# Spreading late weight loads, deeper output and row buffers, two PSUM bank moves and a split last copy in an attention-plus-experts kernel

## The chip, the cores and the metric

One Trainium2 chip, one core. The metric is the device time of one execution in microseconds (us), lower is better. Times come from repeated executions; a profile is one execution with the hardware profiler on, and its span (first to last instruction) is about 1.8 us shorter than the time of the same execution. Most executions of one kernel lie close together.

## The reference, cut to what matters

```python
# attention: batch 4, 8 heads, 768 positions, head_dim 64; each query sees 8 global keys and 96 local ones,
# with a distance bias per head; softmax; then the heads are laid side by side: x is [3072 tokens, 512]
def _moe_ref(x, w_gate, w1, w2):          # 8 experts, w1 [8,512,1024], w2 [8,1024,512]
    cap = N // E                          # 384 tokens for each expert, exactly
    logits = x @ w_gate
    order = np.argsort(-logits.flatten()) # best (token, expert) pair first
    ...                                   # greedy: a pair is taken if the token is free and the expert has room
    for e in range(E):
        h = np.maximum(x[mask_e] @ w1[e], 0.0)
        out[mask_e] = h @ w2[e]
```

## The kernel before

Three memories matter: HBM (the chip's large memory), SBUF (the core's working memory) and PSUM (where TensorE's products land, in banks). The kernel runs in three stages: attention (to about 142 us), routing (the selection of 384 tokens for each expert by rounds, to about 175 us; TensorE does early expert work in its gaps), and the expert stage. In the expert stage the rows of an expert are gathered from HBM by index in slabs of 128 (`xe`), transposed on TensorE (`pxe`), copied to SBUF by VectorE (`xT`), multiplied by w1 (`ph`, ReLU on ScalarE into `hT`) and by w2 (`po`), copied to an output buffer by VectorE (`ot`) and scattered to the output rows. Gathers, scatters and the 1 MB weight loads are all issued by GpSimd and share one DMA queue. Experts 0 to 3 have one slab done early and 2 slabs left; experts 4 to 7 have 3 slabs.

```python
    gp = ...tile_pool(name="gp", bufs=9)     # gathered rows xe
    op = ...tile_pool(name="op", bufs=4)     # output buffers ot
    def late_weights(pin=True):              # next pending 1 MB load: w1_5, w2_5, w1_6, w2_6, w1_7, w2_7
        if lates:
            dst, s_ = lates.pop(0)
            ins = nc.gpsimd.dma_start(dst, s_)
            if pin: tc.keep_in_program_order(ins)
    # ... cut ...
    # end of routing: gathers of experts 0 to 3, then two loads
            for e in range(EX):
                gather(e, range(1, TSLAB), False)
            for _ in range(2):
                late_weights(False)
    # ... cut: expert stage, first=True ...
            load_x(0)                        # transposes and row copies of expert 0
            for e in range(N_EXP):
                ahead = 3
                if e + ahead < N_EXP and not (first and e + ahead < EX):
                    gather(e + ahead, slabs(e + ahead))
                if first and e in (2, 3):
                    late_weights()
                    late_weights()
                # up: ph (3 banks), ReLU to hT
                if e + 1 < N_EXP:
                    load_x(e + 1)
                for j, t in enumerate(slabs(e)):
                    po = ps_o.tile([128, DM], FP32, tag="po")         # 3 banks
                    for fc in range(NFC):
                        nc.tensor.matmul(po, lhsT=hT[...], rhs=w2_of(e)[:, fc, :], ...)
                    ot = op.tile([128, DM], FP32, tag="ot")
                    nc.vector.tensor_copy(out=ot, in_=po)
                    scatter(ot, idi[:, ...])
```

One round of the selection, the part that the change touches. `pk` and the counts `pn` lie in one tile, so in one PSUM bank:

```python
            pkn = ps_d.tile([128, 512], FP32, tag="pk")
            pk = pkn[:, 0:256]...
            # TensorE writes pk, then
            pn = pkn[:, 256:257]
            for hf in range(2):
                nc.tensor.matmul(pn, lhsT=nb[...], rhs=ones_bf[:, 0:1], ...)
            nc.scalar.activation(Xe[:, nk : nk + 1], pn, AF.Identity, scale=-1.0, bias=bias232)
            work(0.85)                                   # TensorE's filler: early expert work
            nc.vector.max(out=mx8, in_=pkn[:, 0:256])    # MAX8
            # Xe from mx8 ... then pr on TensorE from Xe
```

The early output of experts 0 to 3 (`down_one`) accumulates in `pos[e] = ps_f.tile(..., tag="po")`, one bank for all four.

The softmax here doesn't subtract the row's maximum and nothing guards it: scores larger than these inputs give would overflow.

Of the kernel before, what the change touches and what calls it, by code (L numbers as in the profile page):

```python
# [9 lines left out]
FP32 = mybir.dt.float32  # L10
# [10 lines left out]
DM = H_ * D_  # L21
N_EXP = 8
# [6 lines left out]
TSLAB = CAP // 128  # L29
# [16 lines left out]
def kernel(  # L46
# [12 lines left out]
    nc = tc.nc  # L59
# [214 lines left out]
    with ExitStack() as actx:  # L274
# [143 lines left out]
        po = {}  # L418
# [462 lines left out]
    xctx = ExitStack()  # L881
# [7 lines left out]
    w2pool = ctx.enter_context(tc.tile_pool(name="w2pool", bufs=1, reuse_waits="tile"))  # L889
    w_late[2] = w_2  # L890
    late_tiles(w2pool, range(3, N_EXP - 2))
    gp = xctx.enter_context(tc.tile_pool(name="gp", bufs=9, reuse_waits="tile"))
    fp = xctx.enter_context(tc.tile_pool(name="fp", bufs=2, reuse_waits="tile"))
    hp = xctx.enter_context(tc.tile_pool(name="hp", bufs=2, reuse_waits="tile"))
    op = xctx.enter_context(tc.tile_pool(name="op", bufs=4, reuse_waits="tile"))

    def late_weights(pin=True):
        if lates:
            dst, s_ = lates.pop(0)
            ins = nc.gpsimd.dma_start(dst, s_)  # L900
            if pin:
                tc.keep_in_program_order(ins)
# [34 lines left out]
    def early_work(ps_f):  # L937
        hTs, phs, pos = {}, {}, {}
        items = []

        def rows(e):
            def go():
                px = ps_f.tile([128, NKC, 128], BF16, tag="ph", bufs=2, name=f"px{e}")
                for kc in range(NKC):
                    nc.tensor.transpose(px[:, kc, :], xe_early[e][:, 128 * kc : 128 * kc + 128], ident_bf)
                nc.scalar.copy(out=xT_early[e], in_=px)
            items.append((0.25, go))

        def up_one(e, f4, i):
            def go():  # L950
                if f4 == 0 and i == 0:
                    if e % 3 == 0:
                        hTs[e // 3] = hp.tile([128, NFC, CAP], BF16, tag="hT", name=f"hTE{e}")
                if i == 0:
                    phs[e, f4] = ps_f.tile([128, 4, 128], FP32, tag="ph", bufs=2, name=f"phE{e}_{f4}")
                sub, kc = divmod(i, NKC)
                fc = 4 * f4 + sub
                nc.tensor.matmul(phs[e, f4][:, sub, :], lhsT=w1_of(e)[:, kc, 128 * fc : 128 * fc + 128],
                                 rhs=xT_early[e][:, kc, :], start=(kc == 0), stop=(kc == NKC - 1), skip_group_check=True)
                if i == 4 * NKC - 1:  # L960
                    nc.scalar.activation(hTs[e // 3][:, 4 * f4 : 4 * f4 + 4, 128 * (e % 3) : 128 * (e % 3) + 128],
                                         phs[e, f4], AF.Relu)
            items.append((0.078, go))

        def up(e):
            for f4 in range(NFC // 4):
                for i in range(4 * NKC):
                    up_one(e, f4, i)

        def down_one(e, fc):  # L970
            def go():
                if fc == 0:
                    pos[e] = ps_f.tile([128, DM], FP32, tag="po", name=f"poE{e}")
                nc.tensor.matmul(pos[e], lhsT=hTs[e // 3][:, fc, 128 * (e % 3) : 128 * (e % 3) + 128], rhs=w2_of(e)[:, fc, :],
                                 start=(fc == 0), stop=(fc == NFC - 1))
                if fc == NFC - 1:
                    ot = op.tile([128, DM], FP32, tag="ot", name=f"otE{e}")
                    nc.scalar.copy(out=ot, in_=pos[e])
                    nc.gpsimd.memset(nop, 0.0)
                    scatter(ot, idiE[:, e : e + 1])  # L980
            items.append((0.22, go))

        def down(e):
            for fc in range(NFC):
                down_one(e, fc)

        for e in range(EX):
            rows(e)
        for f, e in ((up, 0), (up, 1), (down, 0), (up, 2), (down, 1), (up, 3), (down, 2), (down, 3)):
            f(e)  # L990
        return items

    def routing(general):
      with ExitStack() as dctx:
        dap = dctx.enter_context(tc.tile_pool(name="dap", bufs=1))
        ditp = rpool
        ps_d = dctx.enter_context(tc.tile_pool(name="ps_d", bufs=1, space=bass.MemoryType.PSUM, reuse_waits="tile"))
# [56 lines left out]
        def fast_round(k, X, Dg):  # L1054
            nk = 16 * k
            UB = best(X, Dg)
            pkn = ps_d.tile([128, 512], FP32, tag="pk", name="pkn")
# [8 lines left out]
            for hf in range(2):  # L1066
                nc.tensor.matmul(pk[:, hf, :], lhsT=nb[:, 128 * hf : 128 * hf + 128], rhs=neg_bf,
                                 start=False, stop=True, skip_group_check=True)
            pn = pkn[:, 256:257]
            for hf in range(2):  # L1070
                nc.tensor.matmul(pn, lhsT=nb[:, 128 * hf : 128 * hf + 128], rhs=ones_bf[:, 0:1],
                                 start=(hf == 0), stop=(hf == 1), skip_group_check=True)
            if X is None:
# [7 lines left out]
                out=Xe[:, 0:nk].rearrange("p (c k) -> p c k", k=k),  # L1081
                in0=XM.rearrange("p (c o) -> p c o", o=1).to_broadcast([128, 16, k]),
                in1=mx8[:, 0:k].rearrange("p (o k) -> p o k", o=1).to_broadcast([128, 16, k]),
                op=ALU.mult)
            tok_end()
            pr = ps_d.tile([128, 129], FP32, tag="pr", name="pr")
            nc.tensor.matmul(pr[:, 0 : nk + 1], lhsT=Gm, rhs=Xe[:, 0 : nk + 1], start=True, stop=True)
            prk = ps_d.tile([128, 512], FP32, tag="pr2", name="prk")
            pr2, rk = prk[:, 0:128], prk[:, 128:256]
            nc.tensor.matmul(pr2[:, 0:nk], lhsT=Gm, rhs=Xe[:, 0:nk], start=True, stop=True,  # L1090
                             skip_group_check=True)
            X = begin_X()
# [3 lines left out]
            for k0 in range(0, k, 4):  # L1096
                nc.vector.tensor_tensor(
                    out=tg[:, k0 : k0 + 4, 0:nk],
# [184 lines left out]
        if True:  # L1283
            work(0.7)
            X, Dg = None, None
            for kk in ROUND_KS:
                X, Dg = fast_round(kk, X, Dg)
            best(X, Dg)
            work(1.1)
            mnf = rpool.tile([128, NCHUNK], FP32, tag="mnf", name="mnf")  # L1290
            nc.vector.tensor_tensor(out=mnf, in0=mn, in1=cflag, op=ALU.subtract)
            nc.vector.tensor_tensor(out=M, in0=Ub[:, 8:32, :], in1=bc_e(mnf), op=ALU.is_le)
            dispatch()
            for e in range(EX):
                gather(e, range(1, TSLAB), False)
            for _ in range(2):
                late_weights(False)
            vt = rpool.tile([128, EC, EX], BF16, tag="vt", name="vt")
            for lo_, hi_, at in ((16, 32, 0), (8, 10, 16)):
                n_ = hi_ - lo_  # L1300
                nc.vector.tensor_tensor(
                    out=vt[:, at : at + n_, :], in0=Ub[:, lo_:hi_, 0:EX], op=ALU.is_gt,
                    in1=mn[:, lo_ - 8 : hi_ - 8].rearrange("p (c o) -> p c o", o=1).to_broadcast([128, n_, EX]))
            nc.vector.tensor_tensor(out=vt, in0=vt, in1=Ck, op=ALU.mult)
            work(1.0)
            pf = ps_d.tile([128, 512], FP32, tag="pk", name="pf")
            nc.tensor.matmul(pf[0:1, 0:CE], lhsT=ones_bf[:, 0:1], rhs=Mf, start=True, stop=True, skip_group_check=True)
            nc.tensor.matmul(pf[0:1, CE : CE + EX * EC], lhsT=ones_bf[:, 0:1], rhs=vt.rearrange("p c e -> p (c e)"),
                             start=True, stop=True, skip_group_check=True)
            fc8 = dap.tile([1, N_EXP + 1], FP32)  # L1310
            nc.vector.tensor_reduce(out=fc8[:, 0:N_EXP], in_=pf[0:1, 0:CE].rearrange("p (c e) -> p e c", e=N_EXP),
                                    axis=AX.X, op=ALU.add)
            nc.vector.tensor_tensor(out=fc8[:, 0:N_EXP], in0=fc8[:, 0:N_EXP], in1=capv, op=ALU.subtract)
            nc.vector.tensor_tensor(out=fc8[:, 0:N_EXP], in0=fc8[:, 0:N_EXP], in1=fc8[:, 0:N_EXP], op=ALU.mult)
            nc.vector.tensor_reduce(out=fc8[:, N_EXP : N_EXP + 1], in_=pf[0:1, CE : CE + EX * EC], axis=AX.X, op=ALU.add)
            fm = dap.tile([1, 1], FP32)
            nc.vector.tensor_reduce(out=fm, in_=fc8, axis=AX.X, op=ALU.max)
            nc.vector.tensor_single_scalar(out=fi, in_=fm, scalar=0.0, op=ALU.is_gt)
            while items:
                work(0.1)  # L1320
            while deferred:
                tok_begin()
                tok_end()

    def experts(first):
        with ExitStack() as fctx:
# [23 lines left out]
            for e in range(N_EXP):  # L1350
# [2 lines left out]
                ahead = 3 if first else 2  # L1353
                if e + ahead < N_EXP and not (first and e + ahead < EX):
                    gather(e + ahead, slabs(e + ahead))
                if first and e in (2, 3):
                    late_weights()
                    late_weights()
                hT = hp.tile([128, NFC, CAP], BF16, tag="hT")
                for fc in range(NFC):  # L1360
# [8 lines left out]
                for j, t in enumerate(slabs(e)):  # L1369
                    po = ps_o.tile([128, DM], FP32, tag="po")  # L1370
                    for fc in range(NFC):
                        nc.tensor.matmul(po, lhsT=hT[:, fc, 128 * j : 128 * j + 128],  # L1372
                                         rhs=w2_of(e)[:, fc, :], start=(fc == 0), stop=(fc == NFC - 1))
                    ot = op.tile([128, DM], FP32, tag="ot")
                    nc.vector.tensor_copy(out=ot, in_=po)  # L1375
                    scatter(ot, idi[:, TSLAB * e + t : TSLAB * e + t + 1])

    routing(False)
# [51 lines left out]
```

## Time and profile before

| | before |
|---|---|
| time, median of 4 runs (range) | 277.33 us (276.89 to 279.37) |
| span of the profiled execution (its time) | 274.4 us (276.2) |
| TensorE busy | 245.6 us, 90% |
| expert 5 to expert 6, start to start | 20.76 us |
| expert 6 to expert 7 | 11.07 us |

In the page, the busy row has 40 equal slices of the span with the busy share in tenths; PEclk is the granted clock of TensorE in tenths. From the page of the kernel before:

```profile
span 274.4 us, 7770 instructions
...
PE 245.6 (90%) x3299; PEld 179.0 (65%) x3299; DVE 163.4 (60%) x346; ACT 142.1 (52%) x240; POOL 87.6 (32%) x145
...
PE   8699899999999999999988889979999994499970
...
PEclk9999999999999999999999999999999999599995
```

TensorE is full but for a hole in slices 34 and 35 (226 to 240 us), with a slower clock just behind it. Its timeline there (columns: start us, duration us, engine, line, operation, output<-inputs, shape, count, and in brackets the idle time before it and what ended it):

```profile
223.25 5.36 PE L1363 MATMUL ph<-xT,w 128*128 128x384 bf16 x32
...
237.23 0.59 PE L1341 MATMUL pxe<-ident_bf,xe 128*128 128x128 bf16 x4 [7.73 <-DMA out_dram<-ot,idi]
237.61 6.57 PE L1372 MATMUL po<-w,hT 128*128 128x512 bf16 x22
244.01 5.36 PE L1363 MATMUL ph<-xT,w 128*128 128x384 bf16 x32
...
255.08 5.37 PE L1363 MATMUL ph<-xT,w 128*128 128x384 bf16 x32
```

L1363 with 32 matmuls is one expert's first product: the starts give the step of an expert. The transposes of expert 6 (L1341) wait 7.73 us. The wait is inherited from VectorE, whose timeline says why:

```profile
223.77 1.34 DVE L1375 COPY ot<-po 128x512 f32<-128x512 f32 x2 [4.64 <-DMA out_dram<-ot,idi]
236.15 0.69 DVE L1375 COPY ot<-po 128x512 f32<-128x512 f32 x1 [11.04 <-DMA out_dram<-ot,idi]
236.76 0.74 DVE L1342 COPY xT<-pxe 128x512 bf16<-128x512 bf16 x2
```

An output copy waits 11.04 us for a buffer that an earlier scatter still reads; the row copies (L1342) behind it in VectorE's order wait along, and TensorE waits for them. GpSimd's timeline shows where that scatter stood:

```profile
216.37 0.85 POOL L900 DMA_DIRECT2D w<-in_moe_w_dram  x1
218.69 0.93 POOL L900 DMA_DIRECT2D w<-in_moe_w_dram  x1 [1.46 <-issue]
223.82 1.04 POOL L931 DMA_INDIRECT out_dram<-ot,idi  x1 [4.21 <-DMA out_dram<-ot,idi]
```

The scatter was issued at 223.82 behind two loads; its completion is in the trace at 236.03, 12.2 us later, where scatters in an empty queue need 2.7 us. It had also been issued late: its rows were in the buffer at 211.34 (expert 3's first output copy), but GpSimd, which works in program order, first issued another scatter, three gathers and the two loads and then waited 4.21 us for an earlier scatter, which was itself 13.5 us in the queue (210.19 to 223.65) behind the pair of loads issued at 208.08 and 208.90.

One round of the selection, from the timelines of ScalarE and VectorE: MAX8 waits for ScalarE's read of the counts, though it uses nothing of it.

```profile
152.06 0.26 ACT L1076 ACTIVATE Xe<-pkn,bias 128x1 f32<-128x1 f32 x1
```

```profile
152.35 0.43 DVE L1079 MAX8 mx<-pkn 128x8 f32<-128x256 f32 x1 [0.92 <-ACT Xe L1076]
```

And the end of the kernel:

```profile
260.28 5.34 PE L1372 MATMUL po<-w,hT 128*128 128x512 bf16 x24
...
265.66 0.69 DVE L1375 COPY ot<-po 128x512 f32<-128x512 f32 x1 [1.03 <-PE po L1372]
266.63 0.97 POOL L931 DMA_INDIRECT out_dram<-ot,idi  x1 [0.76 <-DVEq L1387]
```

### The profile page before, as it was taken

How to read it: one execution, taken by the hardware profiler on the slowest of the kernel's cores; microseconds unless marked ns; L12 is line 12 of the kernel's file. 1: busy time of each engine (PE TensorE's matmuls, PEld its weight loads, DVE VectorE, ACT ScalarE, POOL GpSimd, SP SyncE). 2: the span in 40 equal slices, each digit the busy share in tenths (PEclk: the TensorE clock that was granted, in tenths of full speed). 3: DMA queues.
4: the chain of work that ended last, by engine and by line, in shares of the span. 5: the costliest groups of instructions: out<-in, count | busy, mean ns of one | idle time of the engine just before them, and what ended most of it. 6: DMA issues, size and time to landing. Idle time of an engine off the chain costs nothing. (4 is left out here: it accounts for less than half of the span.)

```text
span 274.4 us, 7770 instructions
## 1 busy us (share of the span) xinstructions
PE 245.6 (90%) x3299; PEld 179.0 (65%) x3299; DVE 163.4 (60%) x346; ACT 142.1 (52%) x240; POOL 87.6 (32%) x145
## 2 busy tenths in 40 slices
PE   8699899999999999999988889979999994499970
PEld 2567688888898888878876756656666652145520
DVE  3978998888969887798647677612143210233130
ACT  5998969596895959734332222234333523023500
POOL 5050000020713940050081001478448637141240
PEclk9999999999999999999999999999999999599995
DMA  7993889499597999589969998148976999820321
GB/s 268 327 270 77 205 211 273 85 222 261 124 281 146 237 217 200 127 128 211 209 136 179 208 214 167 60 112 148 191 279 116 186 267 208 279 91 24 117 80 44
DMA packets 52569, 49.29 MB, mean 180 GB/s; under 512 B 29744, under 2 KB 44080, under 8 KB 52528
## 3 DMA queue, kind: packets, MB, share of 16 engines
q0 software_dynamic: 15680, 26.22, 46.4%
q1 hardware_dynamic: 36848, 22.50, 32.5%
q8 instruction: 28, 0.46, 0.8%
q14 instruction: 13, 0.11, 0.1%
HBM read 56.05 MB, written 9.44 MB: 239 GB/s over the span
## 5 line engine op out<-in xcount | busy, mean ns | idle before, releaser
L1366 ACT ACTIVATE hT<-ph 128x256 bf16<-128x256 f32 (+1 forms) x64 | 27.9, 437 | 51.8 <-PE ph L1363 50.1
L400 ACT ACTIVATE P<-ps 128x860 f32<-128x860 f32 (+1 forms) x46 | 39.3, 895 | 23.2 <-PE ps L382 22.5
L382 PE MATMUL ps<-qT,kA 32*128 32x215 f32 (+2 forms) x864 | 43.6, 333 | 2.1 <-ACT qT L347 2.1
L435 PE MATMUL po<-P,v 128*64 128x215 f32 (+6 forms) x576 | 41.5, 293 | 0.3 <-DVE P L415 0.3
L382 PEld LDWEIGHTS ps<-qT,kA 32*128 32x128 f32 x864 | 37.2, 185 | 6.8 <-issue 2.8
L435 PEld LDWEIGHTS po<-P,v 128*64 128x64 f32 x576 | 33.9, 136 | 8.7 <-issue 3.2
L1375 DVE COPY ot<-po 128x512 f32<-128x512 f32 x20 | 13.7, 692 | 43.4 <-PE po L1372 21.1
L415 DVE TENSOR_TENSOR P<-P,Wm 128x860 f32<-128x860 f32 (+1 forms) x32 | 32.9, 1043 | 6.6 <-ACT P L400 3.9
L931 POOL DMA_INDIRECT out_dram<-ot,idi x20 | 19.7, 984 | 37.8 <-DVE ot L1375 31.0
L322 DVE STREAM_TRANSPOSE RT<-RT 128x768 f32<-128x768 f32 x28 | 26.2, 958 | 3.3 <-DMA RT<-in_k_dram 3.3
L466 PE MATMUL pr<-P,onesx 128*32 128x192 f32 (+11 forms) x768 | 27.6, 259 | 0.0
L1372 PE MATMUL po<-w,hT 128*128 128x512 bf16 x112 | 27.3, 397 | 0.0
L1372 PEld LDWEIGHTS <-hT 128*128 128x128 bf16 x160 | 15.6, 100 | 17.5 <-issue 2.2
L466 PEld LDWEIGHTS pr<-P,onesx 128*32 128x32 f32 x768 | 24.7, 109 | 2.3 <-issue 0.3
L1363 PE MATMUL ph<-xT,w 128*128 128x384 bf16 (+1 forms) x160 | 25.1, 316 | 0.0
L332 ACT COPY kA<-RT 128x720 f32<-128x720 f32 (+2 forms) x18 | 24.4, 1354 | 0.1
L1342 DVE COPY xT<-pxe 128x512 bf16<-128x512 bf16 x20 | 7.8, 420 | 24.8 <-PE pxe L1341 24.3
L1363 PEld LDWEIGHTS <-w 128*128 128x128 bf16 x160 | 15.6, 98 | 9.3
L923 POOL DMA_INDIRECT xe<-x_tok,idi x20 | 19.2, 961 | 7.1 <-issue 4.6
L408 DVE TENSOR_TENSOR P<-P,Wm 128x860 f32<-128x860 f32 x16 | 16.4, 1058 | 7.1 <-ACT P L400 7.1
L440 ACT COPY oT<-po 128x384 f32<-128x384 f32 x32 | 14.8, 490 | 11.1 <-PE po L435 11.1
L511 PE MATMUL pk<-ident,oT 128*128 128x128 f32 x96 | 16.5, 288 | 2.1 <-DVE LT L482 2.0
(230 smaller groups left out, 316.4 us busy)
## 6 DMA issues: line engine op xcount, KB each, us to landing
w<-in_moe_w_dram POOLq DMA_DIRECT2D x10, 1024.0 KB, 14.0
v<-in_v_dram SPq DMA_DIRECT2D x32, 180.0 KB, 3.8
RT<-in_k_dram SPq DMA_DIRECT2D x7, 768.0 KB, 4.4
RT<-in_q_dram SPq DMA_DIRECT2D x7, 768.0 KB, 7.3
w_early<-in_moe_w_dram POOLq DMA_DIRECT2D x8, 512.0 KB, 7.9
x_tok<-x SPq DMA_DIRECT2D x32, 96.0 KB, 3.3
RT<-in_moe_w_dram POOLq DMA_DIRECT2D x2, 1024.0 KB, 16.9
w_early<-in_k_dram SPq DMA_DIRECT2D x1, 768.0 KB
```

The lines of the kernel that those rows point to most:

```text
L322: nc.vector.transpose(out=t, in_=src[:, :, 32 * g : 32 * g + 32])
L332: nc.scalar.copy(out=kA[:, i0:i1, 8:128].rearrange("p i (c j) -> p i c j", j=NJ), in_=t[:, i0 * NC5 : i1 * NC5, :].rearrange("p (i c) j -> ...
L382: nc.tensor.matmul(heads[a][:, o : o + w], lhsT=kA[r, gd, i, :], rhs=qTt[r, gd, KT * i : KT * i + w], start=(gd == 0), stop=(gd == 1), ski ...
L400: nc.scalar.activation(P[:, :, 0 : GW[g]], ps[w_][:, :, 0 : GW[g]], AF.Exp, scale=0.125)
L415: tt(out=P[:, :, 0 : GW[g]], in0=P[:, :, 0 : GW[g]], in1=Wm[:, h0 : h0 + 2, lo : lo + GW[g]], op=ALU.mult)
L435: nc.tensor.matmul(po[n][bk][64 * t : 64 * t + 64, a - QB * bk : z - QB * bk], lhsT=v7[:, t, i, :], rhs=P[:, t, o + a - q0 : o + z - q0], ...
L466: nc.tensor.matmul(o_, lhsT=l_, rhs=r_, start=first[gq], stop=True, skip_group_check=True)
L923: ins = nc.gpsimd.indirect_dma_start(out=xe, out_offset=None, in_=x_tok[:, :], in_offset=bass.IndirectOffsetOnAxis(ap=idi[:, s : s + 1], a ...
L931: s = nc.gpsimd.indirect_dma_start(out=out[:, :], out_offset=bass.IndirectOffsetOnAxis(ap=ids, axis=0), in_=ot, in_offset=None)
L1363: nc.tensor.matmul(ph[:, 0 : 128 * ns], lhsT=w1_of(e)[:, kc, 128 * fc : 128 * fc + 128], rhs=xT_e[:, kc, 0:ns, :].rearrange("p t n -> p (t ...
L1366: nc.scalar.activation(hT[:, fc, 0 : 128 * ns], ph[:, 0 : 128 * ns], AF.Relu)
L1372: nc.tensor.matmul(po, lhsT=hT[:, fc, 128 * j : 128 * j + 128], rhs=w2_of(e)[:, fc, :], start=(fc == 0), stop=(fc == NFC - 1))
```

## The change

The intent: no burst of loads in the queue in front of scatters; more buffers, so that a late scatter holds up nobody; MAX8 free of ScalarE; no wait of expert 3's early accumulator for expert 2's copy; the last copy shared by two engines.

```diff
-    gp = xctx.enter_context(tc.tile_pool(name="gp", bufs=9, reuse_waits="tile"))
+    gp = xctx.enter_context(tc.tile_pool(name="gp", bufs=11, reuse_waits="tile"))
-    op = xctx.enter_context(tc.tile_pool(name="op", bufs=4, reuse_waits="tile"))
+    op = xctx.enter_context(tc.tile_pool(name="op", bufs=6, reuse_waits="tile"))
@@ early output of experts 0 to 3
-                    pos[e] = ps_f.tile([128, DM], FP32, tag="po", name=f"poE{e}")
+                    pos[e] = ps_f.tile([128, DM], FP32, tag="pt" if e == 2 else "po", name=f"poE{e}")
@@ one round of the selection
-            pn = pkn[:, 256:257]
+            prk = ps_d.tile([128, 512], FP32, tag="pr2", name="prk")
+            pr2, rk, pn = prk[:, 0:128], prk[:, 128:256], prk[:, 256:257]
@@ (the allocation of prk further down goes)
@@ end of routing
-            for _ in range(2):
-                late_weights(False)
+            late_weights(False)
@@ expert stage
-                if first and e in (2, 3):
-                    late_weights()
+                if first:
                     late_weights()
@@
-                    nc.vector.tensor_copy(out=ot, in_=po)
+                    if e == N_EXP - 1 and t == TSLAB - 1:
+                        nc.vector.tensor_copy(out=ot[:, 0 : DM // 2], in_=po[:, 0 : DM // 2])
+                        nc.scalar.copy(out=ot[:, DM // 2 : DM], in_=po[:, DM // 2 : DM])
+                    else:
+                        nc.vector.tensor_copy(out=ot, in_=po)
```

More of the change, by code (lines that the diff above doesn't have):

```diff
@@ L1087, in fast_round @@
             nc.tensor.matmul(pr[:, 0 : nk + 1], lhsT=Gm, rhs=Xe[:, 0 : nk + 1], start=True, stop=True)
-            prk = ps_d.tile([128, 512], FP32, tag="pr2", name="prk")
-            pr2, rk = prk[:, 0:128], prk[:, 128:256]
             nc.tensor.matmul(pr2[:, 0:nk], lhsT=Gm, rhs=Xe[:, 0:nk], start=True, stop=True,
```

## The prediction

> **What bounds the kernel now.** Time 277.3 us, profiled span 274.4. The engine table has TensorE busy 245.6 us (90%); the 40 slices show it near full except at 230-237 us and in the last slices. The chain of waits is useless here (two pieces, 0.5%), so I read the timeline of TensorE. From 182 us on it runs expert after expert without a gap, except one idle stretch of 7.73 us before 237.23 (released, says the trace, by an output scatter). One expert of 3 slabs takes 11.07 us (starts at 212.18, 223.25; 244.01, 255.08), but from 223.25 to 244.01 it takes 20.76: 9.7 us lost, of which about 1.7 is half clock after the pause (clock records: 0.5 from 234.1 to 241.0; 22 matmuls took 6.57 us instead of 4.91).
>
> Why: VectorE's timeline has an output copy that waits 11.04 us for the scatter that last used its buffer (4 buffers, next to a 4.64 us wait just before); the row-transposing copies for the next expert stand behind it in order, and TensorE behind those. That scatter was issued at 223.82 and landed at 236.03, against 2.7 us in an empty queue, because two weight loads (1 MB each, about 6 us of queue time each, issued 216.4 and 218.7) were ahead of it in the one GpSimd queue. The Trainium skill (DMA: Bandwidth & Descriptors, "Two DMAs through the same engine are not ordered") says descriptors of a queue start in order; the landings here agree.
>
> **The change.**
> 1. Late loads one by one, behind each expert's gathers, and 6 output buffers. I replayed the queue by hand (estimate: weights 6 us, scatter 0.65, gather 0.33, and the eight-deep reuse of completion semaphores): weights of experts 6 and 7 land near 210, 218, 226 and 235, and are wanted from about 232, 237, 243 and 248; no output copy waits for a scatter. Gain 9.7 us, all on TensorE's path.
> 2. Row counts in another bank. MAX8 in each of 4 selection rounds now waits for the ScalarE read of the same bank (0.76 to 0.95 us idle, released by ScalarE); the built program makes it wait for TensorE instead. It saves one handover and a 0.26 us activation: about 0.35-0.4 us a round, 1.4 us in all. TensorE idles 0.35-0.71 us for this chain in each round, so it counts.
> 3. Expert 2's early accumulator in another bank: TensorE's 0.67 us wait at 178.7 goes.
> 4. Last copy in halves. Both halves read one bank. The Trainium skill (PSUM — Partial Sum Buffer, "PSUM bank collisions raise a hardware error") says two engines must not read one bank at once; the built program agrees: the ScalarE half waits for VectorE. They run in series: estimate 0.43 + 0.38 + handover 0.1 against 0.69, so 0.2 us lost.
> 5. Two more row buffers: gathers of expert 4 no longer wait for TensorE; nothing on the path.
>
> Sum: 9.7 + 1.4 + 0.7 - 0.2 = 11.6 us.
>
> **Predicted: 265.7 us, range 263.5 to 268.5.** Faster by over 2% 0.95, within 2% 0.04, slower 0.01.
>
> **What the profile would show.** Span near 262.8. Every 3-slab expert 11.1 us apart, no TensorE wait above 1 us after 182; no half clock before the end. VectorE's wait for scatters gone from the list of waits (15.7 us now). MAX8 released by TensorE, gathers starting near 174.1 instead of 175.6. The last copies one after the other, TensorE's end to last scatter about 0.2 longer. Busy times of engines nearly unchanged.
>
> **What would make it wrong.** A late weight arriving late (the last one has about 13 us of slack by the replay); a new stall of GpSimd on a completion semaphore held by a weight load, which delays scatters or gathers; selection gains swallowed by TensorE's fillers (then 1.4 less); a new clock drop.

## The result, and the profile after

| | before | after |
|---|---|---|
| time, median of 4 runs (range) | 277.33 us (276.89 to 279.37) | 264.25 us (264.06 to 264.95) |
| span of the profiled execution (its time) | 274.4 (276.2) | 262.4 (264.23) |
| expert 5 to 6, start to start | 20.76 | 11.07 |
| first gather issued | 175.59 | 174.05 |
| TensorE's end to the last scatter's start | 1.01 | 1.14 |

The ratio is 0.9519 (95% interval 0.9469 to 0.9569). A ratio is the mean time of one kernel's runs over the mean of the other's of the same rounds, so it is not quite the ratio of the medians quoted. Executions over 1.5% slower than the fastest of the same kernel are left out of the means.

From the page of the changed kernel:

```profile
span 262.4 us, 7770 instructions
...
PE 243.1 (93%) x3299; PEld 178.4 (68%) x3299; DVE 163.4 (62%) x346; ACT 142.6 (54%) x241; POOL 87.1 (33%) x145
...
PE   8699979999999999999998899998999999999960
...
PEclk9999999999999999999999999999999999999996
```

The hole is gone and so is the slow clock. TensorE's timeline (line numbers are a few lower than before: L1360 is the first product, L1339 the transposes, L1369 the second product):

```profile
220.88 5.36 PE L1360 MATMUL ph<-xT,w 128*128 128x384 bf16 x32
...
226.98 0.38 PE L1339 MATMUL pxe<-ident_bf,xe 128*128 128x128 bf16 x4
227.20 4.91 PE L1369 MATMUL po<-w,hT 128*128 128x512 bf16 x22
231.95 5.36 PE L1360 MATMUL ph<-xT,w 128*128 128x384 bf16 x32
```

The transposes of expert 6 wait for nothing, the 22 matmuls behind them take 4.91 us instead of 6.57, and every expert of three slabs takes 11.07 us (starts at 209.81, 220.88, 231.95 and 243.02). No output copy of VectorE waits for a scatter any more, and MAX8 is released by TensorE (timeline of VectorE):

```profile
151.59 0.43 DVE L1080 MAX8 mx<-pkn 128x8 f32<-128x256 f32 x1 [0.41 <-PE prk L1072]
...
228.70 0.69 DVE L1376 COPY ot<-po 128x512 f32<-128x512 f32 x1 [0.87 <-PE po L1369]
```

The end: ScalarE's half starts when VectorE's is over.

```profile
248.22 5.34 PE L1369 MATMUL po<-w,hT 128*128 128x512 bf16 x24
...
253.60 0.42 DVE L1373 COPY ot<-po 128x256 f32<-128x256 f32 x1 [1.04 <-PE po L1369]
254.06 0.37 ACT L1374 COPY ot<-po 128x256 f32<-128x256 f32 x1 [5.15 <-DVE ot L1373]
254.70 0.97 POOL L931 DMA_INDIRECT out_dram<-ot,idi  x1 [0.89 <-ACT ot L1374]
```

Between the two profiles 12.0 us went: 9.69 in the step from expert 5 to 6 (20.76 to 11.07), 1.54 before the first gather (175.59 to 174.05), 0.83 at the early accumulator (its last matmuls start 2.37 us earlier, 178.73 to 176.36, less the 1.54), and 0.13 was lost at the last copy. The sum is 11.93.

### The profile page after: what moved, and what is told of

The parts are those of the page before. It is cut to its first block, busy times and chain, and to the rows that moved or that the text cites. A ratio compares the mean times of both kernels' runs of the same rounds, so it can differ in the third digit from the quotient of the medians.

```text
span 262.4 us, 7770 instructions
## 1 busy us (share of the span) xinstructions
PE 243.1 (93%) x3299; PEld 178.4 (68%) x3299; DVE 163.4 (62%) x346; ACT 142.6 (54%) x241; POOL 87.1 (33%) x145
## 4 chain that ended last, share of the span: by engine, by line
PE 61%; DVE 17%; issue 9%; ACT 4%; POOL 4%; DMA 2%; POOLq 0%; SPq 0%; DVEq 0%
PE po L435 11%; PE ps L382 10%; PE ph L1360 9%; PE po L1369 7%; PE pr L466 7%; DVE RT L322 4%; PE pk L511 4%; DVE P L415 4%; POOL out_dram L931 4%; PE poE L974 3%; DMA RT<-in_q_dram 2%; PE pr L469 2%; DVE qT L347 2%; PE phE L958 1%; PE pxe L1339 1%
## 5 line engine op out<-in xcount | busy, mean ns | idle before, releaser
L1376 DVE COPY ot<-po 128x512 f32<-128x512 f32 x19 | 13.1, 691 | 24.8 <-PE po L1369 23.9
L1369 PEld LDWEIGHTS <-hT 128*128 128x128 bf16 x160 | 15.2, 98 | 16.2
L1369 PE MATMUL po<-w,hT 128*128 128x512 bf16 x112 | 25.6, 379 | 0.0
L1360 PE MATMUL ph<-xT,w 128*128 128x384 bf16 (+1 forms) x160 | 25.1, 315 | 0.0
L1360 PEld LDWEIGHTS <-w 128*128 128x128 bf16 x160 | 15.7, 98 | 9.3
```

The costliest lines, as they stand in the source:

```text
L1360: nc.tensor.matmul(ph[:, 0 : 128 * ns], lhsT=w1_of(e)[:, kc, 128 * fc : 128 * fc + 128], rhs=xT_e[:, kc, 0:ns, :].rearrange("p t n -> p (t ...
L1369: nc.tensor.matmul(po, lhsT=hT[:, fc, 128 * j : 128 * j + 128], rhs=w2_of(e)[:, fc, :], start=(fc == 0), stop=(fc == NFC - 1))
```

## The experiments

All outputs are right. A call ran on one chip; the records number the chips 14, 10, 4 and again 10 (that of the first comparison above is not on record). Each call has its own runs of the kernel before.

### First call: the parts, each alone on the kernel before (chip 14)

Kernel before: 277.16 us, median of 11 (275.98 to 278.86).

**Loads one per expert, all else as before.**

```diff
-            for _ in range(2):
-                late_weights(False)
+            late_weights(False)
@@
-                if first and e in (2, 3):
-                    late_weights()
-                    late_weights()
+                if first:
+                    late_weights()
```

> The kernel before with the late loads one per expert, still 4 output buffers and all else as before. My replay of the queue (theory A: the stall needs a burst of loads AND a shallow ring of output buffers, so taking either away ends it): scatters of expert 3 land near 227, the output copy of expert 4 that reuses their buffer waits about 4 us on VectorE, but TensorE does not wait; the full 9.7 us come back: 267.6 us, ratio 0.965. Theory B (buffers are the cause, loads only secondary): most of the stall stays, at least 5 us of it, 272 us or more. In both the waits of MAX8 stay as before.

Measured: 266.39 us (266.28 to 267.71), ratio 0.9622 (0.9585 to 0.9659). TensorE's steps are 11.07 us each, here from expert 5 to expert 6:

```profile
223.44 5.36 PE L1361 MATMUL ph<-xT,w 128*128 128x384 bf16 x32
...
234.51 5.36 PE L1361 MATMUL ph<-xT,w 128*128 128x384 bf16 x32
```

VectorE still waits for scatters, as the replay said, but for 4 and 5.5 us, and it is through with both copies 1.6 and 1.3 us before TensorE has the next rows for it:

```profile
226.79 0.69 DVE L1373 COPY ot<-po 128x512 f32<-128x512 f32 x1 [4.18 <-DMA out_dram<-ot,idi]
...
237.50 1.31 DVE L1373 COPY ot<-po 128x512 f32<-128x512 f32 x2 [5.54 <-DMA out_dram<-ot,idi]
```

**Six output buffers, all else as before.**

```diff
-    op = xctx.enter_context(tc.tile_pool(name="op", bufs=4, reuse_waits="tile"))
+    op = xctx.enter_context(tc.tile_pool(name="op", bufs=6, reuse_waits="tile"))
```

> The kernel before with 6 output buffers, loads in pairs as before. Theory A: expert 4's copies reuse buffers of scatters that landed before the pair of loads (near 205 and 206) or just behind the first pair (223.7); TensorE's stall goes too, 267.6 us, ratio 0.965; some VectorE waits of 2 to 4 us remain in expert 5. Theory C (the burst of loads in the queue is the cause whatever the buffers): the stall moves by one expert and at least half of it stays, 272 us or more.

Measured: 267.55 us (266.68 to 267.70), ratio 0.9642 (0.9602 to 0.9683). The steps are 11.07 us here too (224.30, 235.37, 246.44). The late scatter is still there: it landed at 236.47, 12.2 us after its issue, and only one wait of VectorE for it is left (GpSimd's timeline, then VectorE's):

```profile
224.22 1.04 POOL L931 DMA_INDIRECT out_dram<-ot,idi  x1 [4.74 <-DMA out_dram<-ot,idi]
```

```profile
236.59 1.34 DVE L1375 COPY ot<-po 128x512 f32<-128x512 f32 x2 [3.78 <-DMA out_dram<-ot,idi]
```

So either part alone removes TensorE's stall, and neither "it is the buffers" (theory B) nor "it is the burst of loads" (theory C) is right: the stall needs both a burst in front of a scatter and so few buffers that a copy soon meets that scatter. Together the two parts bring no more in this stage than one of them; the second is a reserve. With buffers alone the margin is thin: the copy that stalled before now starts at 224.51 and reuses a buffer whose scatter landed at 224.01. The 1.2 us between the two medians is in large part not the stall: the trace of this run has a half-clock period near the start (9.9 to 13.3 us) that the one of the loads run lacks, and its runs without it (266.68 and 266.76) lie 0.3 to 0.4 us above 266.39 (which runs have it is read from the recorded clock, see below).

**Row counts in the other bank, all else as before.**

```diff
-            pn = pkn[:, 256:257]
+            prk = ps_d.tile([128, 512], FP32, tag="pr2", name="prk")
+            pr2, rk, pn = prk[:, 0:128], prk[:, 128:256], prk[:, 256:257]
```

> The kernel before with only the row counts in the other bank. Theory: MAX8 waits for TensorE instead of ScalarE's read, 0.4 us less in each of 4 rounds, and TensorE's path takes it: the first gather is issued 1.5 us earlier, 275.7 us, ratio 0.994. Rival: the early start is eaten by the stall at expert 5, which is paced by the DMA queue and not by TensorE: gather earlier by 1.5 us but time within 0.5 us of before.

Measured: 276.35 us (274.95 to 277.47), ratio 0.9976 (0.9936 to 1.0017): by time alone not told from no change. By the trace MAX8's wait fell in each round (0.76, 0.92, 0.79, 0.95 us in the kernel before; 0.38, 0.41, 0.41, 0.57 here), the first gather was issued at 174.10 instead of 175.59 and expert 5 started at 221.75 instead of 223.25, 1.5 us earlier. Then the stall took some of it: it ended 1.07 us earlier (236.16 against 237.23), and expert 6 started 1.13 us earlier, not 1.5. (The 8.38 us in the line below overstate it: a matmul just before, of about 0.2 us, has no record in this trace.) From TensorE's timeline:

```profile
236.16 0.58 PE L1340 MATMUL pxe<-ident_bf,xe 128*128 128x128 bf16 x4 [8.38 <-DVE xT L1341]
...
242.88 5.36 PE L1362 MATMUL ph<-xT,w 128*128 128x384 bf16 x32
```

**Expert 2's early accumulator in another bank, all else as before.**

```diff
-                    pos[e] = ps_f.tile([128, DM], FP32, tag="po", name=f"poE{e}")
+                    pos[e] = ps_f.tile([128, DM], FP32, tag="pt" if e == 2 else "po", name=f"poE{e}")
```

> The kernel before with only expert 2's early accumulator in another bank. Theory: TensorE's 0.67 us wait at 178.7 goes, the experts start 0.7 to 0.85 us earlier; 276.5 us, ratio 0.997. Rival, as in the run of the row counts: the queue paces the stall, so the pause grows by what was gained and the time stays within 0.3 us of before.

Measured: 276.64 us (275.32 to 278.88), ratio 0.9994 (0.9945 to 1.0043), by time not told from no change. Expert 5 started at 222.56, 0.7 us earlier; the stall ended at 236.70, 0.5 us earlier; but expert 6 started at 244.45, 0.4 us later than in the kernel before. The loss came from the clock: the records show half clock for 10.2 us (232.1 to 242.4) instead of 6.8, and the 22 matmuls behind the stall took 7.53 us instead of 6.57:

```profile
236.70 0.58 PE L1341 MATMUL pxe<-ident_bf,xe 128*128 128x128 bf16 x4 [8.11 <-DMA out_dram<-ot,idi]
...
244.45 5.36 PE L1363 MATMUL ph<-xT,w 128*128 128x384 bf16 x32
```

The time fits the rival, its mechanism only in part. In this trace the stall gave back under 0.2 us of the 0.7, and the longer half clock behind it cost 1.0. In the run of the row counts the stall gave back 0.4 of 1.5. In the changed kernel, with no stall, the part brings its 0.83 us.

### Second call: the last copy and one more bank (chip 10)

Kernel before: 278.93 us, median of 11 (276.07 to 280.20).

**The changed kernel again.**

> The changed kernel itself, as the yardstick for the three beside it: 264.2 us. Every theory expects little spread between its runs (under 1 us), as nothing on TensorE's path waits for the DMA queue any more.

Measured: 274.72 us (273.18 to 276.38), ratio 0.9867 (0.9813 to 0.9920). It is 10.5 us slower than in the first comparison. My expectation missed, the spread of under 1 us included (3.2 us). The trace is the same as the first one's up to 137 us. Then TensorE has pauses that no record explains: about 2.6 us between 138 and 143 us, and about 6 us in the first product of expert 0, which took 3.65 us before:

```profile
182.88 2.18 PE L1360 MATMUL ph<-xT,w_early 128*128 128x256 bf16 x16
186.54 0.60 PE L1360 MATMUL ph<-xT,w_early 128*128 128x256 bf16 x4 [1.47 <-ACT hT L1363]
189.41 1.01 PE L1360 MATMUL ph<-xT,w_early 128*128 128x256 bf16 x4 [2.28 <-ACT hT L1363]
190.87 1.87 PE L1360 MATMUL ph<-xT,w_early 128*128 128x256 bf16 x8 [0.45 <-ACT hT L1363]
```

The waits name ScalarE, but ScalarE waited for TensorE in turn: the semaphore that tells of TensorE's second group of this product rose at 186.08, 1.7 us after the modelled end of its matmuls at 184.35. Both stretches are those in which GpSimd issues a row of gathers. Half clock follows from 189.3 us for 3.4 us.

**The last copy whole again.**

```diff
-                    if e == N_EXP - 1 and t == TSLAB - 1:
-                        nc.vector.tensor_copy(out=ot[:, 0 : DM // 2], in_=po[:, 0 : DM // 2])
-                        nc.scalar.copy(out=ot[:, DM // 2 : DM], in_=po[:, DM // 2 : DM])
-                    else:
-                        nc.vector.tensor_copy(out=ot, in_=po)
+                    nc.vector.tensor_copy(out=ot, in_=po)
```

> The changed kernel with the last copy whole again, on VectorE. Theory: the halves run in series, since both read one bank, so undoing them gains: from TensorE's end to the start of the last scatter 1.01 us instead of 1.14, time 0.1 us lower (264.1). Rival (the intent of the change, halves in parallel): undoing them costs 0.3 us.

Measured: 274.35 us (274.15 to 274.96), beside 274.72 for the changed kernel on the same chip; the pauses spread the times too much to tell 0.1 us. The trace does tell: 1.00 us from TensorE's end (263.89) to the last scatter's start (264.89), as in the kernel before, against 1.14 with the halves. The intent of the halves fails, by 0.13 us, because the two copies read one bank and run one after the other.

**The last slab in two banks, ScalarE's half first.**

```diff
+                    last = e == N_EXP - 1 and t == TSLAB - 1
+                    for n0, n1 in ((0, DM // 2), (DM // 2, DM)) if last else ((0, DM),):
+                        po = ps_o.tile([128, DM], FP32, tag="po")
+                        # 8 matmuls into po[:, 0 : n1 - n0] with rhs=w2_of(e)[:, fc, n0:n1]
+                        if last and n0 == 0:
+                            nc.scalar.copy(out=ot[:, n0:n1], in_=po[:, 0 : n1 - n0])
+                        else:
+                            nc.vector.tensor_copy(out=ot[:, n0:n1], in_=po[:, 0 : n1 - n0])
```

> The changed kernel with the last slab's output computed as two halves of 256 columns in two banks, ScalarE copying the first while TensorE computes the second. Theory: with two banks the wait goes; TensorE's end to the last scatter's start about 0.75 us instead of 1.14, at about 0.05 us more TensorE time: 0.3 us faster than the changed kernel (263.9). Rival (the handover between engines, not the bank, costs the time): no gain over the changed kernel.

Measured: 274.43 us (273.98 to 275.84), no difference to the 274.72 that these runs could tell. Its trace has 1.23 us from TensorE's end to the last scatter's start, not 0.75.

**Expert 3's early accumulator in a third bank.**

```diff
-                    pos[e] = ps_f.tile([128, DM], FP32, tag="pt" if e == 2 else "po", name=f"poE{e}")
+                    pos[e] = ps_f.tile([128, DM], FP32, tag={2: "pt", 3: "pr2"}.get(e, "po"), name=f"poE{e}")
```

> The changed kernel with expert 3's early accumulator in the bank of the selection's row counts too. The first transposes of the expert stage wait 0.67 us for ScalarE's copy of that accumulator. Theory 1: they wait because they reuse the bank that it lies in; then a different bank removes the wait, 0.67 us faster (263.6). Theory 2: they wait because of the order of ScalarE's work or of the buffer pools, whatever the bank; then the wait stays and the time is 264.2.

Measured: 274.71 us (274.12 to 276.14). The wait is still there (TensorE's timeline), so theory 2 holds and this 0.67 us is not to be had by a bank:

```profile
181.50 0.61 PE L1339 MATMUL pxe<-ident_bf,xe 128*128 128x128 bf16 x8 [0.67 <-ACT otE L978]
```

### Third call: which chip, and the stall once more (chip 4)

Kernel before: 277.25 us, median of 11 (276.35 to 279.12).

**The changed kernel, third time.**

> The changed kernel once more. In the last call it took 274.7 us, 10.5 us more than at first: on that chip TensorE pauses for some 2.6 us near 138 to 143 us and some 7 us near 181 to 191 us, both while GpSimd issues a row of gathers, which no other trace so far shows. Theory P (a property of that chip): on another chip the pauses are gone and the time is 264.2 us, on the same one it is 274.7 again. Theory Q (a second state of the changed kernel that can come on any chip): the pauses can come in some executions and not in others within this one call, so that the single times spread over 264 to 275 us.

Measured: 264.71 us (264.28 to 265.10), ratio 0.9537 (0.9512 to 0.9562). No pauses at the gathers. Within a call the kernels never changed from one behaviour to the other, so the pauses go with the chip (theory P), as far as two calls on it and two elsewhere can tell. The six times fall in two groups, 264.28 to 264.39 and 265.03 to 265.10. The profiled one is of the upper group, and its clock records differ from the first profile's in one entry: half clock from 8.9 to 12.3 us, near the start, which cost 1.0 us (spans 262.4 and 263.4).

**The last slab in two banks, again.**

> The last slab in two banks again, beside the changed kernel on this chip. In the last call its profile put the last scatter 0.4 us closer to TensorE's end if the two banks end the wait, as expected then. On a chip without pauses I expect 0.3 us less than the changed kernel (263.9 against 264.2); the rival (the bank does not matter) expects no difference.

Measured: 264.19 us (263.93 to 265.47), ratio 0.9530, beside 264.71. But five of its six runs are of the lower group of times and only three of the changed kernel's, and the lower groups (263.93 to 264.40 and 264.28 to 264.39) overlap: no gain is shown. The trace agrees:

```profile
248.31 5.36 PE L1372 MATMUL po<-w,hT 128*128 128x512 bf16 x31
...
252.84 0.37 ACT L1375 COPY ot<-po 128x256 f32<-128x256 f32 x1 [3.84 <-PE po L1372]
...
253.71 0.42 DVE L1377 COPY ot<-po 128x256 f32<-128x256 f32 x1 [1.05 <-PE po L1372]
254.90 0.97 POOL L931 DMA_INDIRECT out_dram<-ot,idi  x1 [1.00 <-DVEq L1389]
```

The copies do run apart now, and the last one is over at 254.13, 0.46 us after TensorE's end (253.67). But the scatter starts 0.77 us after that, 1.23 us from TensorE's end, where it starts 0.27 us after the last copy in the changed kernel. My expectation missed: the bank was one wait, and behind it stood another.

**The kernel before, a second trace.**

> The kernel before, for a second trace of it. If the length of its stall at expert 5 differs from one execution to the next (my reading of why its times spread over 3 us while those of the version with loads apart lie within 0.2 us), TensorE's wait there is not 7.7 us again but up to 2 us longer or shorter, and the step from expert 5 to expert 6 differs from 20.76 us by as much. If instead the stall is fixed and the spread has another cause, the step is 20.8 us again. On a chip with the pauses at the gathers, the pauses are there too and the stall is shorter by a good part of them.

Measured: 277.10 us, span 275.3 (a single run, so its state is unknown). TensorE's wait was 8.25 us and the step from expert 5 to 6 was 20.71 us (224.19 to 244.90), the 20.76 of the first trace. So the stall is fixed as far as these two traces tell, and my reading of the spread fell. The 0.9 us between the two spans is already there at 144 us, and again it is a half-clock period near the start (9.4 to 12.8 us), which the first trace of before does not have. The windows view says it (columns: stretch; length; busy time and count of TensorE, its weight loads, VectorE, ScalarE, GpSimd; granted clock; DMA share and GB/s), first trace, then second:

```profile
9.00:13.00 4.00, 3.99 (x72) 3.29 (x76) 4.00 (x7) 4.00 (x7) 0.00 (x0) 1.00 1.16 265
```

```profile
9.00:13.00 4.00, 3.95 (x48) 3.66 (x52) 3.25 (x7) 3.08 (x6) 0.00 (x0) 0.57 1.14 254
```

In the second, TensorE got through 48 matmuls where the first did 72. The mean clock for each single run shows the same groups: the kernel before at 276.2 us or less in the first call has 0.976 or 0.977, its other runs there 0.970 to 0.972; the changed kernel's lower group has 0.989 or 0.990, its upper one 0.983 or 0.984. The difference of 0.006 is one half-clock period of 3.4 us in 275. For the kernel before it need not lie near the start: in the trace of the early accumulator alone, 0.972, it lay behind the stall.

### Fourth call: the last slab once more (chip 10 again)

**Two banks, with ScalarE's half last.**

```diff
-                        if last and n0 == 0:
+                        if last and n0 > 0:
```

> The last slab in two banks, with VectorE copying the first half and ScalarE the last. With ScalarE first, the two copies did run apart (the trace shows ScalarE's while TensorE computed the second half), but the last scatter started 0.77 us after the last copy ended, against 0.27 us in the changed kernel: there GpSimd waited in a separate instruction for VectorE's copy and began the scatter only after it, while the scatter's own wait was for ScalarE. Theory W (which of the two waits the scatter carries itself decides): with ScalarE's half last the separate wait is over early, the scatter starts 0.27 us after the last copy and about 0.75 us after TensorE's end, against 1.14 in the changed kernel and 1.23 in the first try; time 0.4 us below the changed kernel, 263.9 us on a chip without pauses (ratio 0.952). Rival (two waits on two engines always cost the 0.5 us): 1.2 us from TensorE's end again.

Measured: 274.79 us (273.73 to 277.39) against 280.05 for the kernel before (277.46 to 281.51 without one run counted as slow), ratio 0.9826 (verdict: unclear). The chip with the pauses again, so the times can't show 0.4 us. The trace shows the step that was tested:

```profile
261.46 5.36 PE L1372 MATMUL po<-w,hT 128*128 128x512 bf16 x31
...
265.99 0.42 DVE L1377 COPY ot<-po 128x256 f32<-128x256 f32 x1 [0.18 <-PE po L1372]
...
266.86 0.37 ACT L1375 COPY ot<-po 128x256 f32<-128x256 f32 x1 [4.71 <-DVEq L1389]
267.51 0.97 POOL L931 DMA_INDIRECT out_dram<-ot,idi  x1 [0.45 <-ACTq L1389]
```

The scatter starts 0.28 us after the last copy and 0.69 us after TensorE's end (266.82): 0.45 us less than in the changed kernel, 0.32 less than in the kernel before. Theory W fits, and the rival does not: in the built program both versions have the same two waits, and only which engine ends last was exchanged. That it is not a matter of ScalarE being quicker to hand over than VectorE is seen in the kernel before, where VectorE's copy ends last, the scatter itself carries the wait, and the gap is 0.28 us too. This is the best ending of all kernels tried; that it makes a faster kernel was not timed on a chip without pauses and stays open.

## Why the prediction was right

The time, 264.25 us, lies in the range (263.5 to 268.5), 1.45 us below the point.

1. *What bounds the kernel.* Right, with one correction. The stall of 9.7 us came from a scatter behind two loads and from the ring of four buffers. I had put both into one step; the runs show that each alone ends it (266.39 and 267.55 us). The part of the argument that said the chain is one of VectorE's order (row copies behind an output copy) is what makes this so: VectorE still waits 3.8 to 5.5 us for scatters in both runs, only not in front of row copies that TensorE needs.
2. *The replay of the queue.* Predicted landings of the loads for experts 6 and 7: 210, 218, 226, 235 us. The trace after has 208.2, 224.9 and 234.5 for the first, third and fourth; the second's completion is not in it, but a scatter queued right behind it landed at 218.2. The last load came 13.7 us before it was used (248.2); predicted were 13.
3. *Selection.* Predicted 1.4 us, measured 1.54; MAX8's waits fell by 0.38 to 0.51 us a round.
4. *Early accumulator.* Predicted 0.7 us, measured 0.83. Alone it brought no time that could be told (ratio 0.9994): in its trace the stall gave back under 0.2 us and a longer half clock behind the stall cost 1.0. In the sum it counts because the stall, and the slow clock with it, is gone. That the small terms could be added to the large one hung on the large one being right.
5. *Last copy.* Predicted 0.2 us lost, measured 0.13 lost. The Trainium skill (PSUM — Partial Sum Buffer, "PSUM bank collisions raise a hardware error") says software must keep two engines off one bank, reads included; the built program does, and the trace shows 0.42 us and 0.37 us one after the other.
6. *Row buffers.* Said to be worth nothing. No run undid them alone, so this stays argued; the other terms sum to 11.93 of the 12.0 us, which leaves little for them.

The term that was off is the starting point, not a mechanism. I subtracted 11.6 us, read from a trace of an execution of 276.2 us, from a median of 277.3. The trace was of the faster group of executions, without the half-clock period near the start; like with like, 274.4 to 262.4, the change brought 12.0 us against 11.6 predicted. The medians differ by 13.1 us, because in the first comparison three of the four runs after (264.06 to 264.26) were of the lower group and none of the four before was below 276.89. The groups come from one more half-clock period in some executions, as far as the traces and the recorded clocks show, near the start or, before the change, perhaps behind the stall; why fewer runs of before fall into the lower group than of the changed kernel is open. The loads alone and the buffers alone agree, like with like: 274.4 to 264.7 without the early period and 275.3 to 265.7 with it, 9.7 and 9.6 us against 9.7 predicted for the stall.

What stays open besides: the pauses on one chip. There the changed kernel takes 274.7 us and the change brings 1.3% instead of 4.6 to 4.8%. The kernel before is only 1.7 to 2.9 us slower on that chip than on the two others (278.93 and 280.05 against 277.16 and 277.25). A possible reason is that its stall takes up the pauses, as it took up part of the gains ahead of it; but no trace of the kernel before was taken on that chip, so this is argued and not shown. What makes TensorE pause is not in the records either.

## What to carry to other kernels

The stall at the shared DMA queue was a chain of three: a burst ahead of a small transfer, a ring of buffers that comes round to that transfer too soon, and an in-order engine that holds other work behind the wait; cutting either of the first two was enough here, and small gains ahead of the stall did not show in the times until it was cut. Splitting the last copy between two engines brought the scatter forward only when the halves lay in different PSUM banks and the wait that was met last was the one that the scatter carried itself (0.69 us against 1.01; 1.14 and 1.23 without one or the other). Compare a trace with the runs of its own group of times, and repeat a result on another chip before a per cent of it is believed.

## What the Trainium skill lacked or had wrong

- DMA: Bandwidth & Descriptors and GPSIMD Engine Reference, as far as I read them: neither has what a scatter's start costs behind its wait. Here it started 0.27 us after the copy when the scatter itself carried the wait that ended last, and 0.77 us after it when a separate wait instruction ended last.
- No page that I read has the pauses of TensorE on one chip beside rows of gathers: 2.6 us at 138 to 143 us and some 6 us between 183 and 195 us, in all five kernels profiled there, and in none of the nine profiles taken in the other calls and the first comparison.
- TensorE: Matmul & The Clock Gate, "What's actually happening", gives two clock states and windows of about 3.4 us. The records agree: 1.0 or 0.5, half-clock periods of 3.4, 6.8 and 10.2 us after a pause. It also says that the slow start differs from run to run, and the traces agree: a half-clock period at about 9 to 13 us comes in some executions and not in others of one kernel, and costs 0.9 to 1.0 us of 275. What it lacks is this form of it, after 3.4 us at full clock, and that groups in the times of one kernel can come from it.
- DMA: Bandwidth & Descriptors, "Two DMAs through the same engine are not ordered": its statement that descriptors of one queue on one DMA engine start in order agrees with every landing read here (scatters 2.7 us in an empty queue, 12.2 us behind two loads). It has no figure for a converting load; a 1 MB load here (float32 in HBM, bfloat16 in SBUF) held the queue for about 6 us (5.2 to 6.1 between landings).
